# Four small products moved from slots 4 to 7 to slots 6 to 9, their rows gathered later, and new ordering constants

## The chip, the cores and the metric

The kernel runs on one core of a Trainium2 chip. The core has five engines that run side by side, each working through its own queue of instructions strictly in order: TensorE (PE, matrix products), VectorE (DVE), ScalarE (ACT), GpSimd (POOL) and SyncE (SP, which here only issues transfers). An instruction waits at the head of its queue until what it reads has been written and what it overwrites has been read; everything behind it waits too. The metric is the device time of one execution in microseconds. Three runs of the kernel before took 943.94, 945.04 and 947.12 us.

## The reference

```python
y  = linear_attention(q, k, v, a_re, a_im)      # 4 batches, 8 heads, 768 steps, head size 48
x  = y.reshape(3072, 384)
h  = x @ w_in                                    # 384 -> 2048
g  = (a0 + a1*h + a2*h2 + a3*h3) / (1 + |b0||h| + |b1|h2 + 1e-6)
x  = g @ w_out                                   # 2048 -> 384, 3072 tokens
e  = argmax(norm(x) @ norm(expert_emb).T / tau)  # one of 8 experts for each token
p  = softmax weight of the chosen expert
out[token] = p * (relu(x[token] @ w1[e]) @ w2[e])   # 384 -> 1024 -> 384
```

All in fp32. With the inputs given, the eight experts get 0, 0, 261, 0, 2, 2798, 9 and 2 of the 3072 tokens.

## The kernel before

Every fp32 product is made of three faster ones: an operand is split in a rounded high part (a cast, written `xh`, `wi_0`, `wo_0`, `gh`) and the rest (`xl`, `wi_1`, `wo_1`, `gl`: the operand minus its high part), and high x high, high x low and low x high are added up in PSUM.

The program has three stages. The attention runs to 252 us and is not touched here. `mixture` holds the other two, and they are one program: `whole()` lists all their operations, and `Plan.emit` puts these into an order before the kernel is built.

**Dense stage.** 64 units: 8 blocks of 384 tokens by 8 pieces of w_in and w_out. A unit is one *up* on PE (18 matmuls of 384 columns, line L1018, into a PSUM tile `ph`), a chain on ACT and DVE for the rational function (ACT L1041, L1042, L1044, L1047, L1048; DVE L1046, L1049, L1050, L1051; then ACT L1052 writes `gh` and DVE L1053 `gl`), and three *downs* on PE (18 matmuls, L1063, into three `acc` banks kept for a block). The high and low parts of the last 11 weight pieces are made in the first units (`split(n)`: L210 the cast, L212 the subtraction); the pieces before were split under the attention. `route(b)` picks the experts of each finished block.

**Slots.** The routed tokens are worked on in 12 slots of 256 tokens of one expert each. A slot has its rows gathered by POOL (L1358), transposed by PE (L1376), split (ACT L982, DVE L1381); 4 ups (L1018, 18 matmuls of 256 columns), each followed by ACT's relu (L1449, `gh`) and DVE's `gl` (L1450); 8 downs (L1461); a scaling on ACT (L1466); a scatter by POOL (L1418). `slot_split(s, q)` makes the high part (L982) and the low part (L1414) of the four quarters of w1 and w2, anew for every slot, in buffers that `chunk(s, q)` picks: 8 sets, but only 6 in the slots from 3 up to the last one that has a small product beside it (the other two hold the small products' weights). In the same slots `work` uses two of the four PSUM halves for its ups. `load(s)` (L1342) fetches an expert's 2 x 1.5 MB of weights, and transfers nothing where the slot's expert is that of the slot before; with these inputs slots 0 to 10 belong to one expert and slot 11 to another, so the loads of slots 0 and 11 are the real ones. Tables that say which tokens go to which slot are made by chains of tiny DVE operations on one partition (L993: `slot_table`, then `half_table` and `next_table`).

**Small products.** Experts with few tokens get one product of 32 rows each, four in all, each beside one slot (`BESIDE`). `mini_gather` has POOL fetch all their rows (L1535), PE transpose them into an `acc` bank (L1548) and ACT copy them. `mini(m, ...)` is an up (L1563), a transpose (L1567), a down (L1573) and a last small product (L1581); `mini_load` fetches its weights.

**What sets the order.** `Plan.add` records an operation with the engines that may do it and an estimated duration on each, what it reads and writes, a bank that it takes or gives, and a `due` time. `emit` walks through time with a clock per engine: of the operations that could start within `slack` (here `SPREAD`) of the earliest it takes the one that is due first, counted back from what depends on it. Where an operation has a choice of engines, it takes the one with the lowest `price` x duration that ends before the operation is late (its due time less `margin`), or, if none does, the one that ends first with a `bias` per engine added (after the time `start`). `COST`, `LEAN`, `SPREAD`, `EARLY_BY` and `LEAN_FROM` are these prices, biases, slack, margin and start for `mixture`. `UNIT` and `GROUP` are the spacing of the units' and the slots' due times, `LAG` how many units after its up a down is due, `AHEAD` how long before its slot a weight split is due, `BEFORE` the same for the rows' low parts. The lines that matter most:

```python
add([("A", 0.73), ("V", 0.47)] if not lo else [("V", 0.87), ("G", 1.76)], ...)   # split(n): high, low
add([("V", 0.87), ("G", 1.76)], ...)                                            # slot_split: low part
return n % 6 if NEARLY <= s < BESIDE.stop else (n + (2 if s >= BESIDE.stop else 0)) % 8   # chunk
```

Of the kernel before, what the change touches and what calls it, by code (L numbers as in the profile page):

```python
# [19 lines left out]
B, H, S, D = 4, 8, 768, 48  # L20
# [11 lines left out]
NBLK = NT // BLK  # L32
# [4 lines left out]
NEARLY = 3  # L37
# [6 lines left out]
NMINI = 4  # L44
# [253 lines left out]
BIAS = {'A': -0.0773127, 'G': 0.1603192, 'V': 0.6045377, 'T': 0.0, 'S': 0.0}  # L298


COST = {'A': 0.7094815, 'G': 0.3193946, 'V': 1.1, 'T': 0.0, 'S': 0.0}
LEAN = {'A': 0.1119026, 'G': 0.1802717, 'V': 0.4995443, 'T': 0.0, 'S': 0.0}
SPREAD = 0.0605191
EARLY_BY = -0.9788931
LEAN_FROM = 4.5359957
MOE = SimpleNamespace(price=COST, bias=LEAN, margin=EARLY_BY, start=LEAN_FROM, chain=0.0, warm=WINDOW, port=True, lat=0.13)
T_PRICE = {'A': 0.738999, 'G': 0.3270214, 'V': 1.1, 'T': 0.0, 'S': 0.0}
T_BIAS = {'A': 0.2620971, 'G': -0.0930716, 'V': 0.822616, 'T': 0.0, 'S': 0.0}
# [7 lines left out]
class Plan:  # L316
# [10 lines left out]
    def add(self, on, fn, r=(), w=(), lat=None, due=1e9, take=None, give=None, dma=0.0, port=True, rush=0.0):  # L327
        n = len(self.ops)
        deps = {self.last[key] for key in (*r, *w) if key in self.last}
        for key in w:  # L330
            deps.update(self.readers.pop(key, ()))
            self.last[key] = n
        for key in r:
            if key not in w:
                self.readers.setdefault(key, []).append(n)
        self.ops.append(SimpleNamespace(
            on=[on] if isinstance(on, tuple) else on, fn=fn, deps=deps - {n}, lat=self.knobs.lat if lat is None else lat,
            due=due, take=take, give=give, dma=dma, port=port, rush=rush, then=None, succ=[], ready=0.0,
        ))
        return n  # L340
# [599 lines left out]
def mixture(tc, ctx, cst, cc, misc, ident, cp, hold, wfp, parts, xs, xT, cnt, idl, x2d, w1, w2, out, coef, bad, safe, stage):  # L940
    nc = tc.nc
    V, A, G, T, SY = nc.vector, nc.scalar, nc.gpsimd, nc.tensor, nc.sync
    eng = {"A": A, "V": V, "G": G, "T": T, "S": SY}
    NP = NF // 2
    NQ = NF2 // 2
    UNIT, GROUP = 6.0000, 16.4000
    LAG = 6.0
    FIRST = 2
    DELAY = -0.4256865
    RAMP = 1.5  # L950
    LATER = 1.0
    AHEAD = 6.0
    BEFORE = 8.0
    FETCH = 0.0

    pool = lambda n: ctx.enter_context(tc.tile_pool(name=n, bufs=1))
    tp, xs.pool = pool("m_t"), pool("m_x")
# [20 lines left out]
    add = lambda *a, due=1e9, **k: st.plan.add(*a, due=due + st.delay, **k)  # L978
# [8 lines left out]
    def chain(calls, key, r=(), first=(), last=(), lat=0.14, due=1e9, rush=0.0):  # L987
        for n, (name, args, kw) in enumerate(calls):
            o = kw["out"] if "out" in kw else args[0]
            size = 1  # L990
            for x in (kw["in0"] if "in0" in kw else kw["in_"] if "in_" in kw else o).shape[1:]:
                size *= x
            add(("V", 0.065 + 0.00105 * size), lambda e, name=name, args=args, kw=kw: getattr(V, name)(*args, **kw),  # L993
                r=list(r) if not n else (), w=[key, *(first if not n else ()), *(last if n == len(calls) - 1 else ())], lat=lat, due=due, rush=rush)
# [25 lines left out]
    def unit(b, i):  # L1020
# [33 lines left out]
        for t in range(TPB):  # L1054
# [9 lines left out]

            add(("T", 0.98), mm2, r=kg + kl + wkey("o", i), w=[key], take=("C", key) if not i else None, due=UNIT * (n + LAG - max(4 - n, 0) * RAMP) + 0.997 * (t + 1))

# [255 lines left out]
    x2k = lambda n: [("x2d", b, t) for b in range(n) for t in range(TPB)]  # L1322

    LAST = NEARLY + NSURE
    turn4 = lambda s: s % 4
    BESIDE = range(NEARLY + 1, NEARLY + 1 + NMINI)

    def cols(s):
        t, n = (tab0, s) if s < NEARLY else (tab, s - NEARLY)
# [69 lines left out]
    def slot_split(s, q):  # L1399
# [6 lines left out]
        for nm, k, src, v, o in (("i", 0, s1, v1, 0), ("o", 1, s2, v2, 2)):  # L1406
            def top(e, nm=nm, src=src, v=v, o=o):
# [4 lines left out]

            add([("A", 0.73), ("V", 0.47 if k else 0.87)], top, r=[("raw", k)], w=[("w" + nm, n, 0)] + ([("w" + nm, n, 1)] if anew else []), due=st.start(s) + 4.0 * (q + 0.5 * k) - AHEAD)
            add([("V", 0.87), ("G", 1.76)], lambda e, src=src, v=v, o=o: eng[e].tensor_tensor(out=v(wset(s, q)[o + 1]), in0=src, in1=v(wset(s, q)[o]).bitcast(F32), op=ALU.subtract),  # L1414
                r=[("raw", k), ("w" + nm, n, 0)], w=[("w" + nm, n, 1)], due=st.start(s) + 4.0 * (q + 0.5 * k) - AHEAD + 2.0)

# [103 lines left out]
    mid = hid[7]  # L1520
# [19 lines left out]
    def mini_gather():  # L1540
        add(("S", 10.0), mini_ids, r=[("tab", 3), *kidl], w=["midt"], lat=1.9, dma=0.4)
        vop(lambda: merge(V, mid, hidt[7]), r=["midt"], w=["mid"], d=0.14, lat=0.2)
        add(("G", 1.04), mini_rows, r=["mid"] + x2k(NBLK), w=[("row", 0)], lat=1.9, dma=0.55)
        key = ("tr", "m")

        def turn(e):
            for k in range(KT):
                T.transpose(bank(key)[:, k * P:(k + 1) * P], names.hx[:, k * P:(k + 1) * P], ident)  # L1548

        add(("T", 0.33), turn, r=[("row", 0)], w=[key], take=("C", key))  # L1550
        add([("A", 0.46), ("V", 0.47)], lambda e: copy(e, names.x, bank(key)[:, :DM].rearrange("p (k n) -> p k n", k=KT)), r=[key], w=[("row", 3)], give=key)
# [39 lines left out]
    def calls(fn, *a):  # L1591
        c = Calls()
        fn(c, *a)
        return c

    def whole():
        st.plan = Plan({"C": range(4)}, MOE)
        st.start = lambda s: UNIT * (NP * NBLK + 0.5) + GROUP * s + min(max(s - BESIDE.start, 0), NMINI) * 4.0
        add(("S", 0.0), lambda e: None, w=["free"], lat=9.0)
        for n in range(NHELD, len(PARTS)):  # L1600
            split(n)
        for b in range(NBLK):
            if b + 1 < NBLK:
                xsplit(b + 1)
            if b == NBLK - 2:
                chain(calls(early_table, 0, 2), "tb", r=["cnt"], first=["xT"], last=[("tab", 0)], due=st.start(0) - 30.0)
                load(0)
                gather(0)
                gather(1)
            elif b == NBLK - 1:  # L1610
                chain(calls(early_table, 2, 1), "tb", r=["cnt"], last=[("tab", 1)], due=st.start(2) - 30.0)
                trans(0)
                gather(2)
            for i in range(NP):
                unit(b, i)
            route(b)
        for s in range(LAST):
            if s > 2:
                gather(s)
            if s:  # L1620
                load(s)
                trans(s)
            for q in range(NQ):
                slot_split(s, q)
            if s == 1:
                chain(calls(slot_table), "tb", r=["cnt"], last=[("tab", 2)], due=st.start(3) - 20.0, rush=0.2)
# [120 lines left out]
```

## Time and profile before

| | |
|---|---|
| median of three runs | 945.04 us |
| the profiled execution | 946.07 us |
| its span, first to last instruction | 944.2 us |
| mean granted clock of TensorE | 0.973 |
| PE busy | 877.2 us, 93% of the span |
| DVE, ACT, POOL busy | 738.1, 704.3, 237.1 us |

The profiled execution is 1.9 us longer than its span, and 1.0 us longer than the median. A share of busy time says which engine comes nearest to having no gap; where the gaps are, and which instruction ends each, has to be read stage by stage.

### The profile page before, as it was taken

How to read it: one execution, taken by the hardware profiler on the slowest of the kernel's cores; microseconds unless marked ns; L12 is line 12 of the kernel's file. 1: busy time of each engine (PE TensorE's matmuls, PEld its weight loads, DVE VectorE, ACT ScalarE, POOL GpSimd, SP SyncE). 2: the span in 40 equal slices, each digit the busy share in tenths (PEclk: the TensorE clock that was granted, in tenths of full speed). 3: DMA queues.
4: the chain of work that ended last, by engine and by line, in shares of the span. 5: the costliest groups of instructions: out<-in, count | busy, mean ns of one | idle time of the engine just before them, and what ended most of it. 6: DMA issues, size and time to landing. Idle time of an engine off the chain costs nothing. (4 is left out here: it accounts for less than half of the span.)

```text
span 944.2 us, 16850 instructions
## 1 busy us (share of the span) xinstructions
PE 877.2 (93%) x6119; PEld 834.0 (88%) x6119; DVE 738.1 (78%) x1419; ACT 704.3 (75%) x1134; POOL 237.1 (25%) x184
## 2 busy tenths in 40 slices
PE   2999999989879999999999999999998979999994
PEld 2788988878779999999999999999998878788994
DVE  7989998989799879787978888796987866556530
ACT  7989998989586988888988888888653543545530
POOL 2425434555254110001001010101322232225311
PEclk9999999989889999999999999999999998999997
DMA  9989988884200000010100000033202156551400
GB/s 174 200 174 175 184 187 175 151 188 100 85 1 1 1 26 1 1 26 1 26 1 26 1 27 1 16 77 94 35 9 60 51 163 204 171 168 37 168 26 27
DMA packets 172865, 76.41 MB, mean 81 GB/s; under 512 B 140840, under 2 KB 167352, under 8 KB 172772
## 3 DMA queue, kind: packets, MB, share of 16 engines
q1 hardware_dynamic: 168804, 65.58, 31.4%
q0 software_dynamic: 3968, 9.66, 3.6%
q8 instruction: 50, 0.82, 0.4%
q14 instruction: 43, 0.35, 0.2%
HBM read 92.19 MB, written 9.96 MB: 108 GB/s over the span
## 5 line engine op out<-in xcount | busy, mean ns | idle before, releaser
L1018 PE MATMUL ph<-xh,wi 128*128 128x384 f32 (+1 forms) x1284 | 306.2, 317 | 8.3 <-DVE wfi L490 4.2
L1018 PEld LDWEIGHTS ph<-xh,wi 128*128 128x128 f32 x1284 | 223.7, 190 | 10.3 <-DVE wfi L490 4.4
L1063 PE MATMUL acc<-wo,gh 128*128 128x392 f32 x768 | 202.0, 344 | 4.1 <-ACT gh L1052 4.1
L1018 PE MATMUL ph<-xl,wi 128*128 128x384 f32 (+1 forms) x642 | 203.1, 316 | 0.0
L1063 PEld LDWEIGHTS acc<-wo,gh 128*128 128x128 f32 x768 | 141.2, 190 | 4.4 <-ACT gh L1052 4.4
L1063 PE MATMUL acc<-wo,gl 128*128 128x392 f32 x384 | 131.7, 343 | 2.5 <-DVE gl L1053 2.5
L1018 PEld LDWEIGHTS ph<-xl,wi 128*128 128x128 f32 x642 | 122.0, 190 | 0.0
L1126 POOL DMA_INDIRECT idl<-tok,pos x24 | 24.6, 1026 | 281.4 <-DVE pos L1123 177.4
L1063 PEld LDWEIGHTS acc<-wo,gl 128*128 128x128 f32 x384 | 72.7, 189 | 3.3 <-DVE gl L1053 3.3
L1461 PE MATMUL acc<-wo,gh 128*128 128x384 f32 x256 | 70.0, 354 | 3.4 <-DVE wo L1414 3.4
L1053 DVE TENSOR_TENSOR gl<-u,gh 128x768 fp32r<-128x768 f32 x48 | 47.0, 979 | 27.1 <-PE acc L1063 26.2
L1041 ACT ACTIVATE sq<-ph,quad 128x768 f32<-128x768 f32 x43 | 38.8, 902 | 30.3 <-PE ph L1018 27.3
L1449 ACT ACTIVATE gh<-ph 128x512 fp32r<-128x512 f32 x36 | 21.6, 599 | 52.6 <-PE ph L1018 31.3
L1461 PEld LDWEIGHTS acc<-wo,gh 128*128 128x128 f32 x256 | 45.8, 194 | 9.1 <-issue 4.6
L499 ACT COPY qkT<-bank 96x512 f32<-96x512 f32 x96 | 50.7, 587 | 3.4 <-PE bank L621 3.0
L1418 POOL DMA_INDIRECT out_dram<-ah,ido x24 | 27.3, 1137 | 99.5 <-ACT ah L1466 55.2
L1358 POOL DMA_INDIRECT xT<-x2d,ids x24 | 27.2, 1134 | 98.9 <-DVE oh L1104 45.9
L630 PE MATMUL bank<-qkT 96*128 96x128 f32 x384 | 50.7, 279 | 1.3 <-ACT qkT L499 1.3
L1046 DVE SCALAR_TENSOR_TENSOR u<-u,qtmp,ph 128x768 f32<-128x768 f32 x47 | 47.2, 1005 | 5.4 <-ACT u L1044 5.3
L620 PE MATMUL bank<-cst,qf 128*96 128x128 f32 x192 | 48.2, 290 | 2.9 <-ACT qkT L499 2.9
L630 PEld LDWEIGHTS bank<-qkT 96*128 96x128 f32 x384 | 46.9, 193 | 2.8 <-ACT qkT L499 2.5
L1049 DVE SCALAR_TENSOR_TENSOR sq<-sq,quad,ah 128x768 f32<-128x768 f32 x43 | 46.6, 1084 | 0.6 <-ACT ah L1048 0.5
(298 smaller groups left out, 2160.6 us busy)
## 6 DMA issues: line engine op xcount, KB each, us to landing
xT<-in_moe_w_dram SPq DMA_DIRECT2D x24, 1536.0 KB
mw<-in_moe_w_dram SPq DMA_DIRECT2D x32, 384.0 KB
raw<-in_moe_w_out_dram SPq DMA_DIRECT2D x16, 384.0 KB
raw<-in_moe_w_in_dram SPq DMA_DIRECT2D x16, 384.0 KB
x2d<-rows SPq DMA_DIRECT2D x24, 192.5 KB
a_re<-in_a_re_dram SPq DMA_DIRECT2D x24, 192.0 KB
a_im<-in_a_im_dram SPq DMA_DIRECT2D x24, 192.0 KB
k<-in_k_dram SPq DMA_DIRECT2D x24, 192.0 KB
```

Of the source, the lines that this page charges most:

```text
L499: (A.copy if e == "A" else eng[e].tensor_copy)(o, i)
L620: T.transpose(pv[:, i, 0, :], Q[:, 2 * j + i, :], ident)
L630: T.matmul(pb(b)[:, i * P:(i + 1) * P], O[:, i, 1, :], O[:, i, 0, :], start=True, stop=True)
L1018: T.matmul(o, l, r, start=(n == 0), stop=(n == len(steps) - 1))
L1041: add(("A", 0.81 if many else 0.45), lambda e, c=c, h=h: A.activation(z[:, c], h(), AF.Abs, scale=coef.kb), w=kh + kz_)
L1046: add(("V", 0.93 if many else 0.53), lambda e, c=c, h=h: V.scalar_tensor_tensor(out=w[:, c], in0=w[:, c], scalar=coef.d, in1=h(), op0=ALU. ...
L1049: add(("V", 0.93), lambda e: V.scalar_tensor_tensor(out=z, in0=z, scalar=coef.e, in1=s, op0=ALU.add, op1=ALU.mult), r=ks, w=kz_)
L1053: add(("V", 0.87), lambda e: V.tensor_tensor(out=l, in0=w, in1=g.bitcast(F32), op=ALU.subtract), r=kw + kg, w=kl, lat=0.27)
L1063: T.matmul(o, x[:, j, sl], y("o", i)[:, c], start=(i == 0 and j == 0 and k == 0), stop=(i == NP - 1 and j == 1 and k == 2))
L1358: G.indirect_dma_start(out=xg[i][t], out_offset=None, in_=x2d[0:n, :], in_offset=bass.IndirectOffsetOnAxis(ap=ids[i][:, t:t + 1], axis=0), ...
L1418: G.indirect_dma_start(out=out[:, :], out_offset=bass.IndirectOffsetOnAxis(ap=dst, axis=0), in_=src, in_offset=None, bounds_check=NT - 1, ...
L1461: T.matmul(o, x[:, j, sl], w[:, c], start=(q == 0 and j == 0 and n == 0), stop=(q == NQ - 1 and j == 1 and n == 2))
```

## The change

Five constants of the ordering and six due times get new values, `BESIDE` begins two slots later (slot 6 in place of 4, its end 10 in place of 8, so that the reduced set of weight buffers and PSUM halves lasts two slots longer), `mini_gather` is listed with slot 5 in place of slot 1, and the time that the plan reckons with for the rows' landing goes from 1.9 to 4.0. No operation is added or removed.

```diff
-COST = {'A': 0.7094815, 'G': 0.3193946, 'V': 1.1, 'T': 0.0, 'S': 0.0}
-LEAN = {'A': 0.1119026, 'G': 0.1802717, 'V': 0.4995443, 'T': 0.0, 'S': 0.0}
-SPREAD = 0.0605191
-EARLY_BY = -0.9788931
-LEAN_FROM = 4.5359957
+COST = {'A': 0.4040183, 'G': 0.5818748, 'V': 1.1, 'T': 0.0, 'S': 0.0}
+LEAN = {'A': -0.5125890, 'G': 0.2593672, 'V': 0.6452497, 'T': 0.0, 'S': 0.0}
+SPREAD = 0.0404030
+EARLY_BY = -0.3016373
+LEAN_FROM = 3.1556660
...
-    UNIT, GROUP = 6.0000, 16.4000
-    LAG = 6.0
+    UNIT, GROUP = 6.9704659, 12.3393091
+    LAG = 9.0119615
...
-    AHEAD = 6.0
-    BEFORE = 8.0
+    AHEAD = 5.1935258
+    BEFORE = 9.7300805
...
-    BESIDE = range(NEARLY + 1, NEARLY + 1 + NMINI)
+    BESIDE = range(NEARLY + 3, NEARLY + 3 + NMINI)
...
-        add(("G", 1.04), mini_rows, r=["mid"] + x2k(NBLK), w=[("row", 0)], lat=1.9, dma=0.55)
+        add(("G", 1.04), mini_rows, r=["mid"] + x2k(NBLK), w=[("row", 0)], lat=4.0, dma=0.55)
...
             if s == 1:
                 chain(calls(slot_table), ...)
                 chain(calls(half_table) + calls(next_table), ...)
+            if s == BESIDE.start - 1:
                 mini_gather()
```

What the constants do is seen in the order of the instructions. The number at a row's start is its place in the engine's queue; `x3` is three alike.

DVE's queue at the start of the dense stage, before (`wfi` and `wfo` are the full weights of a piece, `wi_0`/`wo_0` their high parts, `wi_1`/`wo_1` the low ones):

```order
448 L210 CAST wi_0_2833<-wfi_162 128x2x384
449 L210 CAST wi_0_2838<-wfi_164 128x2x384
450 L210 CAST wo_0_2867<-wfo_161 128x784
451 L210 CAST wi_0_2869<-wfi_166 128x2x384
452 L1046 SCALAR_TENSOR_TENSOR u_2768<-u_2768,qtmp,ph_2779 128x768
453 L210 CAST wo_0_2883<-wfo_165 128x784
454 L210 CAST wi_0_2895<-wfi_168 128x2x384
455 L1049 SCALAR_TENSOR_TENSOR sq_2766<-sq_2766,quad,ah_2764 128x768
456 L1046 SCALAR_TENSOR_TENSOR u_2769<-u_2769,qtmp,ph_2780 128x768
457 L1050 SCALAR_TENSOR_TENSOR sq_2766<-sq_2766,ah_2764 128x768
458 L1049 SCALAR_TENSOR_TENSOR sq_2767<-sq_2767,quad,ah_2765 128x768
```

and in the changed kernel:

```order
448 L212 TENSOR_TENSOR wi_1_2837<-wfi_162,wi_0_2833 128x2x384
449 L212 TENSOR_TENSOR wi_1_2841<-wfi_164,wi_0_2835 128x2x384
450 L212 TENSOR_TENSOR wo_1_2867<-wfo_165,wo_0_2864 128x784
451 L1046 SCALAR_TENSOR_TENSOR u_2768<-u_2768,qtmp,ph_2779 128x768
452 L212 TENSOR_TENSOR wo_1_2910<-wfo_161,wo_0_2839 128x784
453 L1049 SCALAR_TENSOR_TENSOR sq_2766<-sq_2766,quad,ah_2764 128x768
454 L1046 SCALAR_TENSOR_TENSOR u_2769<-u_2769,qtmp,ph_2780 128x768
455 L1050 SCALAR_TENSOR_TENSOR sq_2766<-sq_2766,ah_2764 128x768
456 L212 TENSOR_TENSOR wi_1_2939<-wfi_166,wi_0_2843 128x2x384
457 L1051 SCALAR_TENSOR_TENSOR u_2768<-u_2768,quad,sq_2766 128x768
458 L1049 SCALAR_TENSOR_TENSOR sq_2767<-sq_2767,quad,ah_2765 128x768
```

The casts L210 have left DVE for ACT (all 11 of this stage: four ahead of ACT's first L1041), and the subtractions L212, which stood in POOL's queue, have come to DVE (all 11). In the slots the subtractions L1414 that POOL had, nine of them, are DVE's as well, and most of DVE's casts L982 are ACT's: POOL's queue holds no tensor operation between 252 us and the end any more, only its transfers.

PE's queue where the small products' rows are transposed (L1548), before:

```order
3839 L1018 MATMUL ph_2780<-xl_2620,wi_0_2464 128x256
3840 L1018 MATMUL ph_2780<-xh_2619,wi_1_2503 128x256
3841 L1376 MATMUL acc_2781<-cst,xT 128x128 x3
3842 L1376 MATMUL acc_2783<-cst,xT 128x128 x3
3843 L1376 MATMUL acc_2782<-cst,xT 128x128 x3
3844 L1376 MATMUL acc_2784<-cst,xT 128x128 x3
3845 L1548 MATMUL acc_2781<-cst,rows_3361 128x128 x3
3846 L1461 MATMUL acc_2783<-wo_0_2883,gh_2771 128x384
3847 L1461 MATMUL acc_2783<-wo_1_2897,gh_2771 128x384
```

and in the changed kernel:

```order
4022 L1461 MATMUL acc_2782<-wo_0_3004,gh3e 128x384
4023 L1461 MATMUL acc_2782<-wo_1_3035,gh3e 128x384
4024 L1461 MATMUL acc_2782<-wo_0_3004,gl3e 128x384
4025 L1548 MATMUL acc_2783<-cst,rows_3329 128x128 x3
4026 L1461 MATMUL acc_2781<-wo_0_3004,gh3e 128x384
4027 L1461 MATMUL acc_2781<-wo_1_3035,gh3e 128x384
4028 L1461 MATMUL acc_2781<-wo_0_3004,gl3e 128x384
```

Before, L1548 stands right behind the transposes L1376 of slots 5 and 6, in one of the four banks that these have filled, and ahead of slot 4's first downs. Now it stands between the two halves of the last downs of slot 5, in a bank that no transpose has just filled. POOL's issue of the rows (L1535) keeps its place in POOL's queue, between the scatters of slots 2 and 3.

DVE's queue at slots 9 and 10, where the weights of slot 11 arrive (`wi_0b`, `wo_0b` and `wi_1b`, `wo_1b` are the two sets that the small products' weights had held), before:

```order
1346 L1450 SCALAR_TENSOR_TENSOR gl2e<-ph_2779,gh_2773 128x2x256
1347 L1414 TENSOR_TENSOR wi_1b<-xT,wi_0b 128x768
1348 L1414 TENSOR_TENSOR wi_1_2547<-xT,wi_0_2532 128x768
1349 L1383 COPY xT<-xT 128x1 x2
1350 L1450 SCALAR_TENSOR_TENSOR gl3e<-ph_2780,gh3e 128x2x256
1351 L982 CAST wo_0b<-xT 128x768
1352 L1414 TENSOR_TENSOR wi_1_2503<-xT,wi_0_2464 128x768
1353 L1414 TENSOR_TENSOR wo_1b<-xT,wo_0b 128x768 x2
1354 L1414 TENSOR_TENSOR wo_1_2324<-xT,wo_0_2183 128x768
1355 L1450 SCALAR_TENSOR_TENSOR gl_2774<-ph_2779,gh_2771 128x2x256
```

and in the changed kernel:

```order
1356 L1450 SCALAR_TENSOR_TENSOR gl_2774<-ph_2779,gh_2771 128x2x256
1357 L1414 TENSOR_TENSOR wi_1_2547<-xT,wi_0_2532 128x768
1358 L1450 SCALAR_TENSOR_TENSOR gl_2775<-ph_2780,gh_2772 128x2x256
1359 L1414 TENSOR_TENSOR wo_1b<-xT,wo_0b 128x768
1360 L1450 SCALAR_TENSOR_TENSOR gl2e<-ph_2779,gh_2773 128x2x256
1361 L1414 TENSOR_TENSOR wo_1b<-xT,wo_0b 128x768
1362 L1414 TENSOR_TENSOR wi_1_2503<-xT,wi_0_2464 128x768
1363 L1414 TENSOR_TENSOR wo_1_2324<-xT,wo_0_2183 128x768
1364 L1414 TENSOR_TENSOR wo_1_2567<-xT,wo_0_2362 128x768
1365 L1450 SCALAR_TENSOR_TENSOR gl3e<-ph_2780,gh3e 128x2x256
```

The `b` sets are taken up two slots later. `wo_1b` (L1414), which needs the last weight load, stood with the `gl` of slot 9 and stands now between the `gl` of slot 10 (L1450), one ahead of `gl2e` and one behind it. The load itself stands later in SP's queue, too, beside slot 9's last downs.

## Rows read from the trace of the kernel before

**Rows 1.** Stretches: length us, then busy us (xinstructions) per engine, PEclk, DMA.

```profile
252.72:313.13 60.41, 51.68 (x252) 49.89 (x253) 54.15 (x54) 43.77 (x58) 23.31 (x10) 0.87 0.02 5
313.13:665.00 351.87, 351.87 (x2007) 351.80 (x2007) 290.04 (x521) 305.60 (x431) 26.50 (x25) 1.00 0.09 22
665.00:772.60 107.60, 100.40 (x690) 98.76 (x688) 83.41 (x261) 51.63 (x88) 29.54 (x24) 0.98 0.21 49
772.60:790.00 17.40, 11.03 (x72) 7.10 (x71) 14.96 (x28) 9.49 (x17) 4.84 (x4) 0.80 0.70 213
790.00:930.43 140.43, 139.38 (x1027) 129.57 (x1026) 69.40 (x108) 65.46 (x107) 40.69 (x31) 1.00 0.38 122
930.43:944.20 13.77, 0.00 (x0) 0.00 (x0) 0.00 (x0) 0.58 (x1) 0.97 (x1) 0.63 0.05 18
```

**Rows 2.** Waits of PE, 252 to 314 us: total us, times, longest.

```profile
PE acc L1063 <- ACT gh L1052: 4.1, 1, 4.1
PE ph L1018 <- DVE gl3s L1046: 1.9, 1, 1.9
```

**Rows 3.** Groups, 252.7 to 313.2 us: xcount, busy us, mean ns, idle before.

```profile
L212 POOL TENSOR_TENSOR wo<-wfo,wo 128x784 fp32r<-128x784 f32 x5 | 11.8, 2360 | 14.2 <-DVE wo L210 14.1
L212 POOL TENSOR_TENSOR wi<-wfi,wi 128x768 fp32r<-128x768 f32 x5 | 11.5, 2326 | 15.9 <-DVE wi L210 15.8
L210 DVE CAST wi<-wfi 128x768 fp32r<-128x768 f32 x5 | 6.0, 1221 | 0.0
L210 DVE CAST wo<-wfo 128x784 fp32r<-128x784 f32 x6 | 5.7, 966 | 0.0
L1049 DVE SCALAR_TENSOR_TENSOR sq<-sq,quad,ah 128x768 f32<-128x768 f32 x6 | 9.3, 1551 | 0.0
L1049 DVE SCALAR_TENSOR_TENSOR gh3s<-gh3s,quad,gl2s 128x768 f32<-128x768 f32 x2 | 2.0, 1008 | 0.0
L1051 DVE SCALAR_TENSOR_TENSOR u<-u,quad,sq 128x768 f32<-128x768 f32 x4 | 5.6, 1394 | 0.0
L1052 ACT CAST gh<-u 128x768 fp32r<-128x768 f32 x5 | 4.1, 824 | 4.5 <-DVE u L1051 4.5
```

**Rows 4.** Timeline of DVE, one row: start us, us, instruction.

```profile
258.09 1.03 DVE L210 CAST wi<-wfi 128x768 fp32r<-128x768 f32 x2
```

**Rows 5.** Groups by line, 665 to 931 us.

```profile
L1414 DVE TENSOR_TENSOR wi<-xT,wi 128x768 fp32r<-128x768 f32 x40 | 37.0, 950 | 1.8 <-ACT wi L982 1.1 <-issue 0.6
L982 ACT CAST wi<-xT 128x768 fp32r<-128x768 f32 x43 | 34.3, 834 | 0.0
```

**Rows 6.** Waits of PE, 660 to 946 us.

```profile
PE acc L1548 <- DVE xl L1381: 6.4, 1, 6.4
PE acc L1461 <- DVE wo L1414: 3.4, 1, 3.4
PE acc L1063 <- DVE gl L1053: 1.6, 1, 1.6
PE acc L1461 <- DVE gl L1450: 1.4, 1, 1.4
```

**Rows 7.** Timeline of DVE, 699 to 716 us, around the first table.

```profile
699.94 0.15 DVE L993 TENSOR_SCALAR xT<-cnt 1x8 f32<-1x8 f32 x1
707.88 0.24 DVE L993 TENSOR_SCALAR xT<-xT 1x13 int32<-1x13 f32 x2
```

**Rows 8.** Timeline of DVE and POOL, 768 to 779 us.

```profile
774.93 3.56 DVE L1414 TENSOR_TENSOR wo<-xT,wo 128x768 fp32r<-128x768 f32 x4
778.41 1.01 DVE L1381 TENSOR_TENSOR xl<-acc,xh 128x384 fp32r<-128x384 f32 x2
770.87 1.02 POOL L1535 DMA_INDIRECT rows<-x2d,hids  x1 [0.31 <-issue]
```

**Rows 9.** Timeline of SP's queue and ACT, 878 to 887 us.

```profile
878.53 0.38 SPq L1342 DMA_DIRECT2D xT<-in_moe_w_dram  x1
885.48 1.57 ACT L982 CAST wi_0b<-xT 128x768 fp32r<-128x768 f32 x2 [0.40 <-DMA xT<-in_moe_w_dram]
```

More of the change, by code (lines that the diff above doesn't have):

```diff
@@ L945, in mixture @@
     NQ = NF2 // 2
-    UNIT, GROUP = 6.0000, 16.4000
-    LAG = 6.0
+    UNIT, GROUP = 6.9704659, 12.3393091
+    LAG = 9.0119615
     FIRST = 2
     DELAY = -0.4256865
-    RAMP = 1.5
+    RAMP = 1.5000000
     LATER = 1.0
-    AHEAD = 6.0
-    BEFORE = 8.0
-    FETCH = 0.0
+    AHEAD = 5.1935258
+    BEFORE = 9.7300805
+    FETCH = 0.0000000
     pool = lambda n: ctx.enter_context(tc.tile_pool(name=n, bufs=1))
```

## The prediction

> **What bounds the kernel now.** The busy shares in the table name PE, at 93%, so the first question is where PE does not run. The view of busy time by stretch answers it [rows 1]. From 313.13 to 665.00 us PE has no gap at all and the full clock: 2007 matmuls in 351.87 us, 0.1753 us each. No order of instructions can make this stretch shorter, only longer. All that can be gained lies in the others. From 252.72 to 313.13 us PE runs 252 matmuls; at 0.1753 us they are 44.2 us of work in 60.41 us, so 16.2 us are lost, as idle time and as a clock of 0.87 of full. In the slots, from 665.00 to 930.43 us, PE idles 7.2 + 6.4 + 1.1 = 14.6 us, and the clock of 0.98 and 0.80 stands for 2.2 + 3.5 = 5.6 us, of which a part falls into the idle time; some 20 us in all. The last 13.77 us hold no matmul: the last slot's scaling, its scatter and the end, the same work in both kernels. So with no loss in the stretches of the mixture the kernel would stand at 946.1 - 16 - 20 = 910 us. That is the floor.
>
> The waits of PE say who ends the gaps. At the start they are ACT's `gh` (4.1 us) and DVE's L1046 (1.9 us) [rows 2]; both end the same chain, of which DVE does the larger part. In the slots there are two large waits, 6.4 us before L1548 and 3.4 us for a weight's low part, and smaller ones of 1.6 and 1.4 us [rows 6].
>
> **The start of the dense stage.** DVE is busy 54.15 of the 60.41 us, and not because it has so much to do [rows 1]. POOL spends 23.3 us there on ten subtractions L212 of 2.33 to 2.36 us, and beside them DVE's instructions stretch [rows 3]. A cast L210 takes 0.52 us where POOL rests (two in 1.03 us [rows 4]) and 1.22 and 0.97 us in the means of this stretch; L1049 1.01 us undisturbed and 1.55 in the mean. The excess is 5 x 0.70 + 6 x 0.45 + 6 x 0.54 + 4 x 0.38 (L1051 against L1049's 1.01) = 11.0 us [rows 3]. ACT meanwhile waits 4.5 us for L1051 [rows 3].
>
> The rows show instructions that grow by up to POOL's whole duration. The Trainium skill ("SBUF — State Buffer", section "SBUF: two separate sides") puts it as an exclusive lock: an instruction of VectorE with two SBUF inputs and one of GpSimd that reads SBUF take a shared pair of ports in turn, each for its whole duration. By that rule the ten subtractions could keep DVE waiting up to 23.3 us, and without them DVE would win twice what the rows say; the trace shows half of that, 11.0 us, and I go by it.
>
> The change takes the subtractions from POOL and gives all 11 to DVE, and DVE's 11 casts to ACT. A low part on DVE takes 0.95 us in the slots (40 of them [rows 5]); that is the nearest row for L212 on DVE, of the same form, and POOL's 2.3 us is the upper bound. DVE: 54.15 - 11.7 (its casts as they ran) - 4.8 (the excess of L1049 and L1051) + 11 x 0.95 = 48.1 us. ACT: 43.77 + 11 x 0.83 (the cast in the slots [rows 5]) = 52.9 us. Four of the casts stand ahead of ACT's first L1041 and lie in time that ACT spends waiting for PE's first up. So ACT, not DVE, sets the end of this stretch. Behind the first up (18 matmuls, 6.3 us at half the clock) stand 52.9 - 3.3 = 49.6 us of work, 56 us together, 4 us less than now, if none of it ran on into the next stretch. Followed instruction by instruction with these durations, where the last ACT work of the units is not waited for by the tenth up, PE has done its ten ups and four downs after 50 us, 10 us less. I take 9, with 4 and 12 as the ends (with 12, only 4 us of loss are left, for the first unit's chain).
>
> From there to 665 us I cost the edit at nothing: DVE and ACT were busy 290 and 306 of 352 us [rows 1], the same instructions stay, and a `LAG` of 9 leaves downs behind more ups, not fewer.
>
> **The slots.** *The small products' rows.* POOL issues L1535 at 770.87 us; PE stands before L1548 from 772.64 to 779.01. What it waits for at the end is not the rows, but its bank: L1381 reads it, and that stands on DVE behind four L1414, 774.93 to 778.4 us [rows 8], with the wait put down to L1381 [rows 6]. In the new order L1548 comes some 27 us of PE's work later (the matmuls between the two places at their durations), in a bank long free, with POOL's issue left where it was. The 6.4 us go, and with them the low clock behind: the stretch 772.60 to 790.00 ran at 0.80, 3.5 us lost on the clock [rows 1], about 2 of them after the wait. Together 8.5 us.
>
> *The table.* The chain of L993 holds DVE from 699.94 to 708.1 us with 41 tiny operations [rows 7], and `gl` and two L1414 come out late behind it: the 3.4 us of PE [rows 6], and about 1 us of clock. Now the chain stands ahead of `gl` of slot 0's third part, and by the durations above that `gl` comes 2 us before PE wants it. Gain 4.5 us. The wait of 1.4 us [rows 6] lies in the second chain, whose operations stand between other work now: 2 us with its clock. The 1.6 us between the stages I leave standing.
>
> *What is late next.* Nine low parts come from POOL to DVE in the slots, 9 x 0.95 = 8.6 us on an engine that is busy 168 of 265 us [rows 1]: hidden on the whole, with a place or two where it is not, 2 us. The last weight load is the tight place. SP issued it at 878.53 us and ACT's cast started at 885.48 after waiting 0.40 us for it [rows 9]: 7 us. The second half of that load is now issued some 10 us of PE's work later, ACT's two casts and DVE's `wo_1b` wait for it at the head of their queues, and behind them stand `gh` and `gl2e` of slot 10. With 7 us they come out 1 to 3 us before PE's downs need them. I cost this at 2 us, from 0 to 6 (a load that takes 3 us longer, and the low clock after it).
>
> The slots thus give 8.5 + 4.5 + 2 - 4 = 11 us, with 4 and 17 as ends. Sum: 946.1 - 9 - 11 = 926 us for a profiled execution, which is 1 us above the median: 925 us.
>
> **The rivals.**
> *ACT sets the start.* For it: 52.9 us of work on a strictly ordered queue. Against it: PE's tenth up needs only what unit 7 has finished. The start then gives 4 us, or 930 us.
> *The end of the slots gives it back.* In slots 8 and 9 a quarter's weights go into six buffers instead of eight, and slot 10 takes those that slot 9 has just left; with the load late as well, each of the four quarters waits a cast and a low part, 0.83 + 0.95 us [rows 5], 7 us, and 3 us of clock: 935 us. Against it: with six buffers from 790 us on PE idled 1.1 us in 140 [rows 1].
> *The wait before L1548 stays.* If the tables or the rows come late, or the bank is again one that DVE frees late, 8.5 us are not won: 934 us.
> *Slower than before.* One mechanism: the low parts, all on DVE's one queue now, come out behind whatever waits there. Slots 6 to 9 have 32 pieces in six buffers and with the small products between them; each that is not ready holds PE for a cast and a low part, 1.8 us. It decides from 12 of 32 pieces on, where the 20 us are eaten up; with 18 the kernel takes 925 + 32 = 957 us. For it: the 3.4 us that PE waits for a weight are for a low part from DVE [rows 6]. Against it: DVE has 40 low parts of w1 already [rows 5], and no wait of PE for one of them is among the four longest [rows 6].
>
> **How the numbers follow.** The forecast of 925 us has 0.62, ACT at the start 0.12, the end of the slots 0.10, the wait that stays 0.06, slower 0.10. What a measurement of this kernel can tell from no change is 0.3%, 2.8 us. The slower case yields 0.08 of slower and 0.02 of the same, and the tails of the others 0.01 and 0.03: faster 0.86, same 0.05, slower 0.09. The range: the floor is 910, and all terms at their good ends give 946 - 12 - 17 - 1 = 916; the rivals of the same sign end at 935, and ACT at the start together with the slots' end makes 940. I take 912 to 941, which leaves the slower case out and a little below.
>
> **What would show it.** POOL without tensor work after 252 us; L210 and L212 on ACT and DVE at 0.83 and 0.95 us; DVE's L1049 and L1051 at 1.01 us from the first unit; the first wait for `gh` shorter than 4.1 us, and the tenth up over by 303 us instead of 313. No wait before L1548. In the slots PE idle for under 8 us, the largest wait near slot 10 or 11, behind ACT's cast of `wo_0b`. Wrong would be: PE idle between 313 and 660 us; L212 on DVE at 2 us; a wait for `wi` or `wo` in most slots from 6 on.

## The result, and the profile after

The changed kernel takes 919.17 us (median of four runs, 916.96 to 921.76), beside 946.08 us for the kernel before on the same chip: a ratio of 0.9721, 95% interval 0.9701 to 0.9742. The forecast was 925 us.

The profiled execution of the changed kernel has a span of 915.2 us, 29.0 less than before. Of these, 2.3 us are not the change's: the first up starts at 250.84 us and not at 253.12, and the attention ahead of it is the same instruction for instruction. In the fourteen kernels profiled here that start lies between 250.7 and 260.1 us, so in what follows a run is judged by its ratio, and places are compared by the length of the mixture (first up to the end of the span): 691.1 us before, 664.4 after, 26.7 less. This stretch, in the view that answers to [rows 1]:

```profile
250.44:301.44 51.00, 48.88 (x257) 47.91 (x258) 43.11 (x52) 47.48 (x63) 0.00 (x0) 0.94 0.02 6
301.44:650.00 348.56, 348.56 (x1988) 348.52 (x1988) 287.21 (x532) 304.45 (x435) 27.25 (x25) 1.00 0.16 24
650.00:901.20 251.20, 249.27 (x1801) 235.86 (x1800) 166.82 (x386) 135.65 (x222) 55.77 (x48) 1.00 0.33 101
901.20:915.20 14.00, 0.02 (x1) 0.00 (x0) 0.00 (x0) 0.58 (x1) 0.97 (x1) 0.65 0.05 18
```

The steady part is without a gap, as before. In the first stretch 257 matmuls at 0.1753 us are 45.1 us of work in 51.0: a loss of 5.9 us where it was 16.2. Behind the steady part PE idles 251.20 - 249.27 = 1.9 us, where it was 14.6, at a full clock. So the start gave 10.3 us and the rest 16.4. The waits of PE at the start, beside [rows 2], of which the first, the end of the attention, was there before as well:

```profile
PE ph L1018 <- DVE wfi L490: 4.2, 1, 4.2
PE ph L1018 <- DVE gl3s L1046: 0.8, 1, 0.8
PE ph L1018 <- DVE u L1046: 0.5, 1, 0.5
PE acc L1063 <- DVE gl L1053: 0.4, 1, 0.4
```

and from the end of the dense stage to the last matmul, beside [rows 6]:

```profile
PE ph L1018 <- DVE wi L1414: 1.6, 1, 1.6
PE ph L1018 <- ACT gh L1449: 0.4, 1, 0.4
```

The wait of 4.1 us for `gh` at the start, the 6.4 us before L1548 and the 3.4 us for a low part of w2 are gone; the 1.6 us between the stages stay, now before an up. The groups of the start, beside [rows 3], with the subtractions on DVE and the casts on ACT:

```profile
L212 DVE TENSOR_TENSOR wo<-wfo,wo 128x784 fp32r<-128x784 f32 x6 | 5.8, 970 | 1.2 <-ACT wo L210 1.1
L212 DVE TENSOR_TENSOR wi<-wfi,wi 128x768 fp32r<-128x768 f32 x5 | 4.7, 955 | 0.3 <-ACT wi L210 0.2
L210 ACT CAST wo<-wfo 128x784 fp32r<-128x784 f32 x6 | 4.9, 872 | 0.0
L1049 DVE SCALAR_TENSOR_TENSOR sq<-sq,quad,ah 128x768 f32<-128x768 f32 x5 | 5.1, 1014 | 0.5 <-ACT ah L1048 0.5
L1051 DVE SCALAR_TENSOR_TENSOR u<-u,quad,sq 128x768 f32<-128x768 f32 x4 | 4.1, 1014 | 0.1
```

L1049 and L1051 are at 1.01 us where their means were 1.55 and 1.39, and the subtraction on DVE takes 0.96 us. The small products' rows, beside [rows 8]: POOL issues them at 754.71 us, 16 us earlier than before ("gathered later" is said of the place in the list of operations; the place in POOL's queue stayed). PE transposes them 24.5 us after that, between two downs and without a wait:

```profile
754.71 1.02 POOL L1535 DMA_INDIRECT rows<-x2d,hids  x1 [0.31 <-issue]
...
779.07 0.34 PE L1461 MATMUL acc<-wo,gl3e 128*128 128x384 f32 x1
779.24 0.49 PE L1548 MATMUL acc<-cst,rows 128*128 128x128 f32 x3
779.49 0.60 PE L1461 MATMUL acc<-wo,gh3e 128*128 128x384 f32 x2
```

The second half of the last weight load, beside [rows 9], the place where the prediction saw a new loss. From above: SP's queue, ACT, DVE.

```profile
867.41 0.38 SPq L1342 DMA_DIRECT2D xT<-in_moe_w_dram  x1
...
875.82 1.57 ACT L982 CAST wo_0b<-xT 128x768 fp32r<-128x768 f32 x2 [3.72 <-SPq L163]
...
877.92 0.69 DVE L1450 SCALAR_TENSOR_TENSOR gl2e<-ph,gh 128x512 fp32r<-128x512 f32 x1 [0.27 <-ACT gh L1449]
```

The cast starts 8.4 us after the issue, where the prediction reckoned with 7. ACT waits 3.7 us for the load at the head of its queue, DVE's `gl2e` comes out at 878.6 us, and PE, which first reads it at 880.3, has no wait in this place.

### The profile page after: what moved, and what is told of

It reads as the page before. It is cut to its first block, busy times and chain, and to the rows that moved or that the text cites. A ratio compares the mean times of both kernels' runs of the same rounds, so it can differ in the third digit from the quotient of the medians.

```text
span 915.2 us, 16860 instructions
## 1 busy us (share of the span) xinstructions
PE 866.2 (95%) x6119; PEld 825.7 (90%) x6119; DVE 722.7 (79%) x1418; ACT 715.6 (78%) x1155; POOL 195.3 (21%) x164
## 5 line engine op out<-in xcount | busy, mean ns | idle before, releaser
L1018 PE MATMUL ph<-xh,wi 128*128 128x384 f32 (+1 forms) x1308 | 309.3, 317 | 7.4 <-DVE wfi L490 4.2
L1018 PEld LDWEIGHTS ph<-xh,wi 128*128 128x128 f32 x1308 | 227.1, 190 | 9.5 <-DVE wfi L490 4.4
L1018 PE MATMUL ph<-xl,wi 128*128 128x384 f32 (+1 forms) x654 | 206.4, 316 | 0.0
L1018 PEld LDWEIGHTS ph<-xl,wi 128*128 128x128 f32 x654 | 124.1, 190 | 0.0
L1053 DVE TENSOR_TENSOR gl<-u,gh 128x768 fp32r<-128x768 f32 x48 | 45.7, 953 | 20.1 <-PE acc L1063 20.1
L1414 DVE TENSOR_TENSOR wo<-xT,wo 128x768 fp32r<-128x768 f32 x46 | 42.5, 950 | 15.0 <-ACT wo L982 15.0
L1041 ACT ACTIVATE sq<-ph,quad 128x768 f32<-128x768 f32 x43 | 38.8, 903 | 19.8 <-PE ph L1018 15.5
L1461 PEld LDWEIGHTS acc<-wo,gh 128*128 128x128 f32 x272 | 47.5, 188 | 4.1 <-issue 3.3
L1418 POOL DMA_INDIRECT out_dram<-ah,ido x24 | 29.3, 1222 | 100.6 <-ACT ah L1466 65.8
L1049 DVE SCALAR_TENSOR_TENSOR sq<-sq,quad,ah 128x768 f32<-128x768 f32 x43 | 43.5, 1011 | 7.0 <-ACT ah L1048 6.9
```

Of the source, the lines that this page charges most:

```text
L1018: T.matmul(o, l, r, start=(n == 0), stop=(n == len(steps) - 1))
L1041: add(("A", 0.81 if many else 0.45), lambda e, c=c, h=h: A.activation(z[:, c], h(), AF.Abs, scale=coef.kb), w=kh + kz_)
L1049: add(("V", 0.93), lambda e: V.scalar_tensor_tensor(out=z, in0=z, scalar=coef.e, in1=s, op0=ALU.add, op1=ALU.mult), r=ks, w=kz_)
L1053: add(("V", 0.87), lambda e: V.tensor_tensor(out=l, in0=w, in1=g.bitcast(F32), op=ALU.subtract), r=kw + kg, w=kl, lat=0.27)
L1418: G.indirect_dma_start(out=out[:, :], out_offset=bass.IndirectOffsetOnAxis(ap=dst, axis=0), in_=src, in_offset=None, bounds_check=NT - 1, ...
L1461: T.matmul(o, x[:, j, sl], w[:, c], start=(q == 0 and j == 0 and n == 0), stop=(q == NQ - 1 and j == 1 and n == 2))
```

## The experiments

In the experiments the kernel before took 947.8 to 951.3 us in the median beside the runs, against 946.1 above; a kernel is therefore compared by its ratio to the runs of the kernel before that were taken beside it. Three measures from the profiled execution stand with the ratio: the length of the mixture; the loss in the first 60 us behind the first up (60 less the matmuls recorded there x 0.1753); and PE's idle time from 640 us to its last matmul. The last row's kernel has the changed kernel's start and shows 5.1 us of loss there where that shows 5.7, so half a microsecond of loss is not to be read. The time behind the last matmul, the same work in all, lies between 13.8 and 15.2 us, so a microsecond of the mixture is not to be read either.

| kernel | ratio to before | mixture, us | loss at the start | idle behind |
|---|---|---|---|---|
| before | 1 | 691.1 | 15.8 | 14.6 |
| after | 0.9721 (0.9701 to 0.9742) | 664.4 | 5.7 | 1.9 |
| engine constants alone | 0.9799 (0.9769 to 0.9829) | 674.0 | 5.1 | 9.7 |
| due times alone | 1.0207 (1.0173 to 1.0240) | 711.2 | 13.2 | 29.2 |
| move alone | 0.9925 (0.9897 to 0.9952) | 688.4 | 15.8 | 12.6 |
| after, old engine constants | 1.0180 (1.0149 to 1.0212) | 710.3 | 13.2 | 27.1 |
| after, not moved | 0.9806 (0.9775 to 0.9837) | 676.3 | 5.1 | 9.7 |
| after, L212 on POOL | 0.9739 (0.9704 to 0.9775) | 666.5 | 6.7 | 1.9 |
| after, L210 on DVE | 0.9737 (0.9695 to 0.9779) | 669.5 | 9.0 | 1.8 |
| after, both | 0.9784 (0.9738 to 0.9829) | 673.5 | 13.5 | 1.8 |
| after, POOL busy, two inputs | 0.9711 (0.9681 to 0.9740) | 666.9 | 6.9 | 1.9 |
| after, POOL busy, one input | 0.9737 (0.9706 to 0.9768) | 666.1 | 5.1 | 1.9 |
| after, PE kept at work | 0.9682 (0.9648 to 0.9716) | 662.8 | 3.2 | 1.6 |
| after, 24 L1414 on POOL | 0.9790 (0.9755 to 0.9826) | 670.5 | 5.1 | 5.3 |

**Which part of the change does it.** First the engine constants alone in the kernel before (all five; `SPREAD` among them sets how far the order may look ahead, the others the choice of engine).

```diff
-COST, LEAN, SPREAD, EARLY_BY, LEAN_FROM = (old)
+COST, LEAN, SPREAD, EARLY_BY, LEAN_FROM = (new)
```

> The kernel before with the five constants that choose engines alone (COST, LEAN, SPREAD, EARLY_BY, LEAN_FROM). POOL's queue has no L212 in the dense stage and few L1414. Theory (the choice of engines makes the gain of the start): PE loses 6 us instead of 16 between the first up and 305 us; in the slots the wait before L1548 stays: 930 to 938 us. Rival (the due times make the gain of the start): 943 to 948 us, the start as before.

The loss at the start falls to 5.1 us: the whole gain of the start belongs to these constants. In the slots two waits for `gl` lead, 2.6 us each in total, and none stands before L1548, against the theory:

```profile
PE acc L1063 <- DVE gl L1053: 2.6, 2, 1.7
PE acc L1461 <- DVE gl2e L1450: 2.6, 1, 2.6
```

Then the due times alone (there are five of them, not six as the text on the change has it):

```diff
-    UNIT, GROUP = 6.0000, 16.4000
-    LAG = 6.0
+    UNIT, GROUP = 6.9704659, 12.3393091
+    LAG = 9.0119615
...
-    AHEAD = 6.0
-    BEFORE = 8.0
+    AHEAD = 5.1935258
+    BEFORE = 9.7300805
```

> The kernel before with the six due times alone (UNIT, GROUP, LAG, AHEAD, BEFORE and what follows from them). POOL's queue has the 11 L212 and many L1414. Theory (without the choice of engines the due times win nothing at the start): the start loses 14 to 18 us, and POOL's L1414 of 2.3 us in the slots make more waits, 940 to 955 us. Rival (the due times make the gain): 925 to 935 us.

Slower than expected at its worst. With the old constants of engine choice POOL gets 48 subtractions L1414, and PE's long waits, between 674 and 779 us, are for DVE; that POOL's work makes DVE late there is argued, not shown:

```profile
PE ph L1018 <- DVE xl L1381: 6.8, 1, 6.8
PE acc L1114 <- DVE oh L1107: 6.6, 1, 6.6
PE ph L1018 <- DVE gl L1450: 5.4, 2, 3.5
```

The changed kernel with the old engine constants tells the same from the other side:

> The changed kernel with the five constants that choose engines set back to the old values; due times and the move stay changed. Theory: the start loses 10 us more than in the changed kernel, and some in the slots, where POOL has many L1414: 929 to 945 us. Rival (the constants of engine choice matter little): 918 to 924 us.

```profile
PE ph L1018 <- DVE xT L993: 8.6, 2, 5.2
PE acc L1461 <- POOL wo L1414: 2.7, 3, 1.7
```

At 1.018 it is slower than before, and worse than expected. PE's waits for POOL's own results are 2.7 us of 27; the long ones end on DVE. The move alone:

```diff
-    BESIDE = range(NEARLY + 1, NEARLY + 1 + NMINI)
+    BESIDE = range(NEARLY + 3, NEARLY + 3 + NMINI)
...
-        add(("G", 1.04), mini_rows, ..., lat=1.9, dma=0.55)
+        add(("G", 1.04), mini_rows, ..., lat=4.0, dma=0.55)
...
+            if s == BESIDE.start - 1:
                 mini_gather()
```

> The kernel before with the move alone: small products beside slots 6 to 9, rows gathered with slot 5, landing reckoned at 4.0; all constants old. Theory: the start keeps its loss of 16 us (POOL has the 11 subtractions), the wait of 6.4 us before L1548 and the low clock behind it go: 935 to 940 us. Rival (the place alone wins nothing, another wait comes in its stead): 944 to 950 us.

```profile
PE acc L1461 <- DVE wo L1414: 6.9, 1, 6.9
```

The wait before L1548 is gone, but the wait for a low part of w2 behind the table's chain grew from 3.4 to 6.9 us. The ratio says 7 us, the mixture's length 2.7: the eight runs fall into two groups, 938.5 to 940.2 and 944.5 to 946.0 us, and the profiled one is the slowest. The move is worth little while that chain stands where it did. The reverse, the changed kernel without the move:

> The changed kernel with the small products back beside slots 4 to 7, their rows gathered with slot 1 and the landing reckoned at 1.9; all constants stay as changed. Theory (the place of L1548 is worth some 8.5 us, the rest of the gain belongs to the constants): a wait of 4 to 7 us before L1548 or the first small product is back, and the kernel takes 924 to 930 us. Rival (the constants alone take the wait away, since DVE's four subtractions before L1381 are moved by them): 918 to 921 us, no wait before L1548.

The ratio is worse by 0.0085, 8 us, though no wait stands before L1548. In the profiled execution, the slowest of its five, the time goes in eleven waits that the changed kernel doesn't have, of 0.4 to 2.0 us, 8.1 us together; two of them in PE's timeline:

```profile
763.72 0.39 PE L1018 MATMUL ph<-xh,wi 128*128 128x256 f32 x1 [1.97 <-DVE gl L1450]
...
810.33 0.83 PE L1581 MATMUL ph<-rows,cst 128*32 128x384 f32 x2 [1.10 <-ACT rows L982]
```

So the rival was right on L1548 and wrong on the time: the constants alone take that wait away, and the move still pays. How it pays stays open: eight of the eleven waits, 5.6 us, come before L1548 (at 772.6 us there), ahead of any small product, and only three, 2.6 us, among the small products, so it is not only that slots 4 to 7 have less to do.

Three of these kernels form a row. The engine constants alone give 0.9799; with the due times 0.9806, no difference that can be read; with the move as well 0.9721. In this order the gain of the start and 4.9 us of PE's idle time in the slots belong to the engine constants, nothing that can be read to the due times, and 7.8 us of idle time to the move. In another order the shares differ: with the due times and the move already in, the engine constants are worth 0.046 (1.0180 to 0.9721), more than twice their 0.020 alone.

**What the start owes to which engine.** Here the order stays that of the changed kernel; only the engine that executes is another.

```diff
-        add(on, lambda e: parts.split(eng[e], i, nm, lo), ...)
+        add(on, lambda e: parts.split(eng["G" if lo else e], i, nm, lo), ...)
```

> The changed kernel with its order untouched, but the 11 subtractions L212 of the dense stage executed by POOL where DVE's queue has them. Theory (POOL's subtractions stretch DVE beside them and come out later, 2.3 us instead of 0.95): DVE's L1049 and L1051 are back at means of 1.3 us and more, PE loses about 10 us more between 250 and 305 us, 927 to 931 us against 919. Rival (the gain of the start came from the 11 casts that went from DVE to ACT, POOL beside DVE costs nothing that PE waits for): DVE is 10 us less busy than in the changed kernel, and the time is 917 to 920 us.

```profile
L212 POOL TENSOR_TENSOR wo<-wfo,wo 128x784 fp32r<-128x784 f32 x6 | 12.4, 2070 | 23.5 <-ACT wo L210 23.3
L1049 DVE SCALAR_TENSOR_TENSOR sq<-sq,quad,ah 128x768 f32<-128x768 f32 x5 | 7.5, 1491 | 3.9 <-ACT ah L1048 3.9
L1053 DVE TENSOR_TENSOR gl<-u,gh 128x768 fp32r<-128x768 f32 x5 | 6.1, 1225 | 0.2 <-ACT gh L1052 0.2
```

DVE's instructions stretch as the theory said, L1049 back to 1.49 us, and it costs 1 us of loss. The theory on PE falls, and the rival is nearer: DVE was rid of the subtractions and had the time, busy 38.7 of the first 52 us, stretching included (44.2 in the changed kernel). The casts back on DVE:

```diff
+        add(on, lambda e: parts.split(eng[e if lo else "V"], i, nm, lo), ...)
```

> The changed kernel with its order untouched, but the 11 casts L210 of the dense stage executed by DVE where ACT's queue has them; the 11 subtractions stay on DVE, POOL rests. The stretch from the first up on loses 5.7 us of PE in the changed kernel, 6.7 with the subtractions on POOL, 15.8 before. Theory A (what counts is that the casts left DVE): DVE gets 11 x 0.55 = 6 us more on a queue that is nearly full, the loss is 8 to 12 us, the time 921 to 926 us at 919 for the changed kernel. Theory B (only casts on DVE and subtractions on POOL together hurt, since the casts are what the shared port stretches most): the loss stays at 6 to 7 us.

```profile
L210 DVE CAST wo<-wfo 128x784 fp32r<-128x784 f32 x6 | 3.3, 558 | 0.0
L210 DVE CAST wi<-wfi 128x768 fp32r<-128x768 f32 x5 | 2.7, 551 | 0.0
```

Undisturbed, 0.55 us each, and the loss is 9.0: 3.3 us more. Then both:

```diff
+        add(on, lambda e: parts.split(eng["G" if lo else "V"], i, nm, lo), ...)
```

> The changed kernel with its order untouched, but casts L210 on DVE and subtractions L212 on POOL, as the kernel before has them. Theory A (casts on DVE): loss in the start 9 to 13 us, most of it as with the casts alone. Theory B (both together): loss 12 to 16 us, as before, with L210 at means near 1 us and L1049 near 1.5. Theory C (it is the order, not the engine): loss under 8 us.

```profile
L210 DVE CAST wi<-wfi 128x768 fp32r<-128x768 f32 x5 | 5.5, 1115 | 0.0
L1051 DVE SCALAR_TENSOR_TENSOR u<-u,quad,gh3s 128x768 f32<-128x768 f32 x1 | 2.6, 2635 | 0.0
PE ph L1018 <- DVE u L1046: 3.5, 2, 3.1
PE acc L1063 <- DVE gl L1053: 2.4, 1, 2.4
```

13.5 us. The subtractions on POOL cost 1.0, the casts on DVE 3.3, both together 7.8, more than the sum. POOL's work now lengthens the casts too (1.1 us in the mean, not 0.55), and DVE, busy 38.7 of the first 52 us with the subtractions alone on POOL, is busy 44.7 here. PE's waits are for DVE and for ACT behind it; none is for POOL's own results. The remaining 2 us to the 15.8 of before are the order's: both kernels with the old engine constants and the new due times lose 13.2. Theory B of the expectations is nearest.

Does POOL's work alone disturb, if nobody waits for it? Behind each L212 on DVE, POOL gets eight pieces of 96 columns, which it reads twice (two inputs) or once:

```diff
+            for c in range(8):
+                at = WO * (c // 4) + 96 * (c % 4)
+                y = x[:, at:at + 96]
+                G.tensor_tensor(out=spareg, in0=y, in1=y, op=ALU.subtract)   # or G.tensor_copy(spareg, y)
```

> The changed kernel with work added that nobody waits for: behind each of the 11 L212 on DVE, POOL makes 8 subtractions of 96 columns with two SBUF inputs (the high part minus itself) into a tile that is never read. Theory (sharing the port alone stretches DVE): DVE's L1049, L1050, L1051 and L212 grow in the mean by 0.2 to 0.6 us in that stretch, DVE's busy time there by 6 to 12 us, the kernel takes 923 to 930 us. Rival (POOL costs only because PE waits for its late results): DVE's instructions keep 0.95 to 1.01 us, and the kernel takes 919 us.

```profile
L1010 POOL TENSOR_TENSOR spareg<-wi 128x96 bf16<-128x96 f32 x32 | 22.2, 693 | 16.7 <-DMA xT<-y 14.3
L1060 DVE SCALAR_TENSOR_TENSOR sq<-sq,quad,ah 128x768 f32<-128x768 f32 x5 | 5.6, 1111 | 0.3 <-ACT ah L1059 0.3
L1064 DVE TENSOR_TENSOR gl<-u,gh 128x768 fp32r<-128x768 f32 x4 | 4.4, 1096 | 0.0
```

(lines of these two kernels are 11 higher: L1060 is L1049, L1064 is L1053)

> As the run with POOL's added subtractions, but each is a copy with one SBUF input, in 8 pieces of 96 columns behind each of the 11 L212. Theory (any work of POOL that reads SBUF takes DVE's second port away): stretched DVE instructions as in that run, less by as much as POOL is busy less, 921 to 928 us. Rival (only two inputs on POOL's side hurt): DVE undisturbed, 919 us.

```profile
L1010 POOL CAST spareg<-wi 128x96 bf16<-128x96 f32 x32 | 19.4, 607 | 16.2 <-DMA xT<-y 14.2
L1060 DVE SCALAR_TENSOR_TENSOR sq<-sq,quad,ah 128x768 f32<-128x768 f32 x5 | 5.1, 1015 | 0.4 <-ACT ah L1059 0.4
L1064 DVE TENSOR_TENSOR gl<-u,gh 128x768 fp32r<-128x768 f32 x5 | 5.1, 1013 | 0.0
```

POOL is busy for 43 of 52 us in both, twice as long as in the kernel before. With two inputs L1049 takes 1.11 us and L1053 1.10, where the changed kernel has 1.01 and 0.95; with one input L1049 takes 1.015, as without, and L1053 1.01. The ratios do not differ from the changed kernel's. Neither theory met its size: these pieces cost DVE a tenth, not the half that whole subtractions of 2 us cost. That it is their smallness is likely but not shown alone: they also write bf16, and read one operand twice where a subtraction reads two.

**What is left at the start.**

```diff
     plan.emit(clock, SLACK)          # end of attention()
+    if not again:
+        x = parts.tiles[0, "i", 0]
+        for _ in range(22):
+            T.matmul(banks[2][:, :DM], x[:, 0:P], x[:, 0:DM], start=True, stop=True)
```

> The changed kernel with 22 matmuls of 384 columns added at the end of the attention, into a PSUM bank that is free there, whose results nobody reads: PE works in the 4.2 us in which it waits before the first up. Theory (the loss that is left at the start is the low clock of the first up): the first up takes 3.2 us instead of 6.3, the loss falls from 5.7 to about 3 us, the whole to 915 to 917 us. Rival (ACT and DVE set the start, a faster first up only lengthens the waits behind): loss 5 to 6 us, 918 to 920 us.

```profile
250.42 4.11 PE L825 MATMUL bank<-wi 128*128 128x384 f32 x22
254.76 0.41 PE L1022 MATMUL ph<-xh,wi 128*128 128x384 f32 x1 [0.23 <-DVE wfi L490]
```

22 matmuls fill PE's wait for the end of the attention, and the first up runs at the full clock. The loss falls from 5.7 to 3.2 us, the granted clock of the first 60 us rises from 0.95 to 1.00, and the ratio is 0.9682: the lowest here, by 0.4% against the changed kernel, but the intervals overlap, so the gain at the start is shown and the gain in the whole time is not yet.

**POOL in the slots.**

```diff
-            add([("V", 0.87), ("G", 1.76)], lambda e, ...: eng[e].tensor_tensor(...
+            add([("V", 0.87), ("G", 1.76)], lambda e, ...: eng["G" if k and q % 2 else e].tensor_tensor(...
```

> The changed kernel with its order untouched, but 24 low parts L1414 of w2 in the slots (the second and fourth quarter of each of the 12 slots) executed by POOL where DVE's queue has them. PE loses 1.9 us between the dense stage and its last matmul in the changed kernel. Theory (POOL's subtraction takes 2.3 us instead of 0.95 and holds up POOL's transfers and DVE beside it, and PE waits for it): 6 to 20 us more, waits of PE's L1461 for POOL's wo among the largest. Rival (in the slots DVE and POOL have time to spare, what cost PE before was the order alone): within 2 us of the changed kernel.

```profile
L1414 POOL TENSOR_TENSOR wo<-xT,wo 128x768 fp32r<-128x768 f32 x23 | 54.7, 2388 | 33.0 <-ACT wo L982 32.9
L1414 DVE TENSOR_TENSOR wo<-xT,wo 128x768 fp32r<-128x768 f32 x23 | 29.0, 1260 | 10.3 <-ACT wo L982 10.3
PE acc L1461 <- DVE gl2e L1450: 2.6, 1, 2.6
...
800.81 4.53 DVE L1414 TENSOR_TENSOR wo<-xT,wo 128x768 fp32r<-128x768 f32 x1
...
800.85 3.67 POOL L1414 TENSOR_TENSOR wo<-xT,wo 128x768 fp32r<-128x768 f32 x2
```

6.1 us more in the mixture, at the lower end of the theory, and not by the way that it named: PE's one new long wait, 2.6 us, is for DVE's `gl2e`, and no wait for POOL's own result is recorded. The low parts of w2 that DVE still makes grew from 0.95 to 1.26 us in the mean, one of them to 4.53 us beside two subtractions of POOL.

## Why the prediction was right, and where not

*Where the loss was.* The floor reckoned from [rows 1] held: the steady part gained nothing and lost nothing, and both stretches around it came close to their work.

*The start, 9 us forecast, 10.3 measured.* The size was right. The prediction put POOL's subtractions beside DVE first and took them and the casts off DVE in one sum. The subtractions on POOL alone cost 1 us in the new order, the casts on DVE alone 3.3, both 7.8. What counts is DVE's queue: the casts on it, and POOL's work that lengthens them and the rest. The figure for DVE (48.1 us) was too high: DVE is busy 43.1 us in the first 51.0. Of the 5.0 us, 3.3 are stretching that the prediction's 11.0 us left out (one more L1051, which took 2.47 us, and the means of 1.17 and 1.10 us of L1053 and L1050 against 0.95); most of the rest is that 52 instructions of DVE fell into the stretch and not 54. That ACT would set the end did not come true either: ACT is busy 47.5 of the 51.0 us, and the three waits left (0.8, 0.5 and 0.4 us) are for DVE. The larger part of what is left is the clock of the first up: 2.5 of the 5.7 us go in the run with PE kept at work, in which the three waits stay.

*The rule on the shared ports.* The rule of the Trainium skill ("SBUF — State Buffer", section "SBUF: two separate sides"), an exclusive lock for whole instructions, gave the prediction an estimate of up to 23.3 us. The rows were the right side to take: with the 3.3 us left out they hold 14.3. Whole subtractions of POOL do look like the rule: an L1051 of 1.01 us took 2.63 us beside POOL with L210 on DVE and L212 on POOL. Copies with one input do not, though the rule names any GpSimd instruction that reads SBUF: POOL was busy with them for 43 of 52 us, in pieces of 0.61 and 0.66 us in the mean, and L1049, with its two inputs, kept 1.015 us, so there the measurement decides. The run with the subtractions alone on POOL shows why no sum of stretched instructions is a time: 6 us of excess on DVE (five each of L1049, L1050 and L1053 in that run), 1 us for PE.

*The slots, 15 us of waits removed and 4 us of new ones forecast; 16.4 net measured.* The three waits went. The term that was mis-sized is the one for what is late next: 4 us were set, 0.4 came. Three small waits of the kernel before that the prediction did not count, 1.9 us together, went as well:

```profile
PE ph L1018 <- DVE wi L1414: 0.8, 1, 0.8
PE ph L1567 <- ACT sq L1576: 0.7, 1, 0.7
PE ph L1581 <- ACT gh3e L1449: 0.4, 1, 0.4
```

The load did make ACT wait (3.7 us) and DVE with it, but the slack of 1 to 3 us that the prediction reckoned to PE held: 1.7 us were left. The nine low parts that came from POOL to DVE were hidden. With 24 of them given to POOL PE idled 3.4 us more and the mixture took 6.1 us more, so they stand better on DVE; what the nine alone are worth was not tried.

*Whose the gain is.* The prediction gave 8.5 us to the move of L1548. The kernel without the move has no wait there, and the kernel with the move alone wins only 3 to 7 us, since the other large wait of DVE's queue grows from 3.4 to 6.9 us. On top of the other constants the move is worth 8 us, close to the 8.5, but by other and smaller waits: that this number agrees is luck. Its rival of a wait that stays did not come, nor its slower case. The due times without the engine constants are slower than before, at 1.02, but not by that case: there POOL, not DVE, had most of the low parts of w1, and PE waited for other results of DVE.

What stays open: how the move saves its 8 us, and the share of the due times in the whole. Alone they cost 20 us, beside the engine constants nothing; how the engine constants and the move do without them was not tried.

## What to carry to other kernels

Where an engine is full in a stage, look for what makes its instructions long before moving them: the casts cost most on the engine that was full, while another engine's work doubled them. Constants that set an order act only together; a part that is slower alone can stand in a faster whole, so judge them by the waits they leave, stage by stage. And an engine that has time to spare takes stretched instructions at little price: here 6 us of stretching on DVE cost PE 1 us.

## What the runs showed of the hardware

At the start one subtraction of POOL with two inputs (means of 2.04 to 2.36 us) lengthened a DVE instruction beside it by up to 1.6 us (2.63 us for an L1051 of 1.01). In the run with POOL in the slots a low part of 0.95 us on DVE took 4.53 us beside two such subtractions in a row, and the delay goes the other way too: one subtraction of POOL, 1.84 us at its shortest, took 7.34 us beside a run of DVE instructions. The same number of columns in pieces of 96, at 0.69 to 0.76 us each in the mean and with POOL busy twice as long, lengthened L1049 by 0.1 us in the mean; copies with one input lengthened L1053 by 0.06 us and L1049 by nothing that can be read.

TensorE's granted clock at the first up followed what PE did just before. Behind a wait of 4.2 us the first up began at 0.50, the lower level (1.2 of 2.4 GHz), with pairs of matmuls at 0.84 us; with matmuls in that wait it ran at 1.00, with pairs at 0.51 us. The views of the two stretches, the changed kernel's first:

```profile
250.84:254.00 3.16, 3.16 (x10) 3.16 (x11) 0.00 (x0) 3.05 (x4) 0.00 (x0) 0.50 0.24 65
254.76:258.00 3.24, 3.24 (x19) 3.24 (x20) 0.00 (x0) 2.99 (x4) 0.00 (x0) 1.00 0.26 68
```
